# Which DMA engine a store leaves out: eleven dV by a table, and pairs of o in two or three parts

## The chip, the cores and the metric

The kernel runs on one core of one Trainium2 chip. The metric is the device time of one execution in microseconds (us); lower is better.

## The reference

The kernel computes attention and its gradients for 32 batches. Each batch has 32 query heads of 4 rows, so 128 rows of 128 elements, and 4 key/value heads of 2048 rows. All tensors are bf16.

```python
def _fwd_reference(q, k, v):            # q (32,32,4,128), k and v (32,4,2048,128)
    k = jnp.repeat(k, rep, axis=1)      # rep = 8 query heads for each key head
    v = jnp.repeat(v, rep, axis=1)
    scores = jnp.einsum("bhqd,bhkd->bhqk", q, k) * D ** -0.5
    p = _softmax(scores, axis=-1)
    return jnp.einsum("bhqk,bhkd->bhqd", p, v)

def reference(q, k, v, grad_out):
    out, vjp = jax.vjp(_fwd_reference, q, k, v)
    return (out, *vjp(grad_out))        # o, dQ, dK, dV
```

K and V are 2 MB each per batch, and so are dK and dV; q, grad_out, o and dQ are 32 KB each. The core reads 136 MB and writes 136 MB.

## The kernel before

One batch is one unit of work. Its 128 query rows lie on the 128 partitions, and K, V, dK and dV lie as 128 partitions of 4 heads by 16 rows by 128 elements: a partition holds 4 KB of each head, which is also contiguous in memory. A DMA of one of these tensors therefore moves rows of 4 KB, one for each partition and head.

The steps of a batch have short names. LK and LV load K and V, four DMAs of 512 KB each, issued by SyncE (lines 153 and 159). QDT, KT and VT turn q, K and V by TensorE's transpose through PSUM; VectorE copies them out (line 182). Sa and Sb compute the scores and their maxima, EXa and EXb the exponentials, NRM the sums, their reciprocals and two scaled operands, `dop` and `qp`, which GpSimd writes (line 230). ETa, ETb, dSTa and dSTb turn the exponentials and dS back. O computes the output and its inner product with grad_out, dPa and dPb compute dS. dV0 to dV7 and dK0 to dK7 (`outer`, lines 295 to 337) each compute an eighth of dV or dK into two PSUM banks, which ScalarE copies (line 310) into an output tile. dQ is the last step.

The order of all steps is written out by hand: HEAD for the first batches, STEADY for a loop body that works on a batch and its neighbours, TAIL for the end. Every engine executes its share in that order. K has three buffers, V two. dV and dK share four output tiles (`out_pool`, tag "outp"), so a tile is written again by the same tensor two batches later, after its store has landed.

Stores are issued by GpSimd through `store` (line 132), behind each other and between its other work; only after the last V load has been issued do they go to SyncE's queue. When the eighth dV or dK of a batch has been copied, its tile is stored at once (lines 326 to 337). Outputs o go out for two batches at a time, at each odd batch (lines 277 to 279). GpSimd also loads q and grad_out for four batches at a time (`GROUP`).

The stores of some batches are split by partitions ("rows" below). A store of 128 rows gives 8 rows to each of the 16 DMA engines. In the code's reckoning a store of fewer rows uses as many engines as the largest number up to 16 that divides its rows: 120 rows use 15 engines, 104 use 13, 88 use 11, 40 use 10, 24 use 12, 8 use 8. Those engines follow each other from a round-robin start, and the next such store starts where the last ended. Before the change dV of batch 0 is stored as 128 rows of two heads, then 88 and 40 rows of the other two, which puts the start at engine 5. At each fourth batch (3, 7, ... 27) dV is stored as 128 rows of one head, then 120 and 8 rows of the other three, and the pair of o before it (from batch 7 on) as 104 and 24 rows, so that the start is at 5 again. The 120 rows of these seven dV leave out engine 4.

Of the kernel before, what the change touches and what calls it, by code (L numbers as in the profile page):

```python
# [40 lines left out]
dV0@-1 dPa@-1 dV3@-1 dK4@-1 dQ@-2 dK3d@-1 dK2@-1 dK0d@-1 dK1@-1 dK5d@-1 dK7@-1 dK6@-1 dSTa@-1 dSTb@-1 dQ@-1  # L41
"""
TAIL_ITERATIONS = 3


class Banks:
# [31 lines left out]
def kernel(ctx: ExitStack, tc: tile.TileContext, q, k, v, grad_out, out_0, out_1, out_2, out_3):  # L78
# [3 lines left out]
    P = 128  # L82
# [38 lines left out]
    o_f = out_0.rearrange("b h s d -> b (h s) d")  # L121
# [3 lines left out]
    dk_v = out_2.rearrange("b h (p c) d -> b p h (c d)", c=C)  # L125
    dv_v = out_3.rearrange("b h (p c) d -> b p h (c d)", c=C)

    st = {}

    def store(**kw):  # L130

        (nc.sync if "v" in st.get(B - 1, {}) else nc.gpsimd).dma_start(**kw)  # L132
# [125 lines left out]
    def gathered(S, xt, kv):  # L258
        t = banks.take(1)
        ps = banks.ap(t)[:, 0, 0:D]  # L260
        for c in range(C):
            for h in range(NH):
                nc.tensor.matmul(  # L263
                    ps[G * h:G * h + G, :], lhsT=S[f"{xt}{c // 8}"][:, c % 8, G * h:G * h + G], rhs=S[kv][:, h, c, :],
                    start=(c == 0), stop=(c == C - 1), tile_position=(0, G * h),
                )
        return t, ps

    def O(b):
        S = st[b]  # L270
        t, ps = gathered(S, "et", "v")
        if b % 2 == 0:
            st["o"] = io_pool.tile([P, 2, D], BF16, name="o_sb")
        o_sb = st["o"][:, b % 2, :]
        nc.vector.tensor_scalar(out=o_sb, in0=ps, scalar1=S["rinv"][:], scalar2=None, op0=ALU.mult)
        banks.give(t)
        if b % 2:
            for r in (slice(0, 104), slice(104, P)) if b % 4 == 3 and b > 3 else (slice(0, P),):
                store(out=o_f[b - 1:b + 1, r].rearrange("w p d -> p w d"), in_=st["o"][r])
        junk = sm_pool.tile([P, D], BF16, name="junk")  # L280
        S["delta"] = sm_pool.tile([P, 1], FP32, name="delta")
        nc.vector.tensor_tensor_reduce(
            out=junk[:], in0=o_sb, in1=S["do"], scale=1.0, scalar=0.0,
            op0=ALU.mult, op1=ALU.add, accum_out=S["delta"][:],
        )
# [9 lines left out]
    def outer(S, x, y, dst, name, i, b, copy):  # L295

        if name not in S:
            S[name + "left"] = 8
            S[name] = out_pool.tile([P, NH, C, D], BF16, name=name, tag="outp")
        t = banks.take(2)  # L300
        ps = banks.ap(t).rearrange("p a (j c d) -> p a j c d", j=2, c=2)
        for c in range(2):
            u = P * ((2 * i + c) % 8)
            for a in range(2):
                r = slice(2 * G * a, 2 * G * a + 2 * G)
                nc.tensor.matmul(  # L306
                    ps[:, a, :, c, :], lhsT=S[f"{x}{i // 4}"][r, u:u + P], rhs=S[y][r, :, :],
                    start=True, stop=True, tile_position=(2 * G * a, 0),
                )
        copy(  # L310
            out=S[name][:, :, 2 * i:2 * i + 2, :].rearrange("p h c d -> p h (c d)"),
            in_=banks.ap(t).rearrange("p a (j w) -> p (a j) w", j=2),
        )
        banks.give(t)
        S[name + "left"] -= 1
        if b == B - 1:

            half = f"{name}half{i // 4}"
            S[half] = S.get(half, 4) - 1
            if S[half] == 0:  # L320
                c = slice(8 * (i // 4), 8 * (i // 4) + 8)
                store(
                    out=dst[b].rearrange("p h (c d) -> p h c d", d=D)[:, :, c, :].rearrange("p h c d -> p h (c d)"),
                    in_=S[name][:, :, c, :].rearrange("p h c d -> p h (c d)"),
                )
        elif S[name + "left"] == 0:
            o = S.pop(name)[:].rearrange("p h c d -> p h (c d)")
            parts = [(slice(0, P), slice(0, NH))]

            if name == "dv" and b == 0:
                parts = [(slice(0, P), slice(0, 2)), (slice(0, 88), slice(2, 4)), (slice(88, P), slice(2, 4))]
            elif name == "dv" and b % 4 == 3:
                parts = [(slice(0, P), slice(0, 1)), (slice(0, 120), slice(1, 4)), (slice(120, P), slice(1, 4))]
            for r, h in parts:
                store(out=dst[b][r, h, :], in_=o[r, h])

    def dV(b, i, copy=nc.scalar.copy):
        outer(st[b], "e", "dop", dv_v, "dv", i, b, copy)  # L340

    def dK(b, i, copy=nc.scalar.copy):
        outer(st[b], "ds", "qp", dk_v, "dk", i, b, copy)

    def dP(b, i):
# [6 lines left out]
        banks.give(t)  # L352

    table = {"LK": LK, "LV": LV, "QDT": QDT, "O": O, "dQ": dQ, "NRM": NRM}
    for i, c in enumerate("ab"):
        for n, f in (("S", S_), ("EX", EX), ("dP", dP), ("ET", ET), ("dST", dST)):
# [8 lines left out]
    for w in STEADY.split():  # L365
        ahead = 0
        for mark, n in (("+3", 3), ("+2", 2), ("+", 1), ("-2", -2), ("-", -1)):
            if w.endswith(mark):
                w, ahead = w[:-len(mark)], n
# [3 lines left out]
    with tc.manual_schedule():  # L373

        for w in HEAD.split():
            w, b = w.split("@")
            table[w](int(b))
        for it in range(HEAD_ITERATIONS, B - TAIL_ITERATIONS):
            for w, ahead in steady:
                if 0 <= it + ahead < B:  # L380
                    table[w](it + ahead)
        for w in TAIL.split():
            w, b = w.split("@")
# [31 lines left out]
```

## Time and profile before

| | |
|---|---|
| time of three runs, median (lowest to highest) | 685.96 us (685.48 to 688.05) |
| the profiled execution: its time | 682.75 us |
| its span from first to last instruction | 680.5 us |
| mean granted TensorE clock | 0.998 |
| TensorE matmul busy | 623.7 us, 92% of the span |
| VectorE, ScalarE, GpSimd busy | 594.5, 563.3, 259.6 us |
| moved by DMA | 274.45 MB, mean 403 GB/s |
| DMAs issued by SyncE, by GpSimd | 269, 140 |

The profile is one execution on the chip. The busy time of an engine is the sum of its instructions. The chain of waits is followed back from the last instruction: at each step to what released it, or to the instruction before it on the same engine. "DMA k_sb<-in_k_dram" in it is time in which the chain waits for a load of K. Queue q1 holds the DMAs issued by SyncE, q0 those issued by GpSimd, q8 and q14 fetch instructions. The DMA share is the mean busy share of the core's 16 DMA engines.

### The profile page before, as it was taken

The page shows a single profiled execution, that of the slowest core. Times are in us where ns is not written, and L with a number is a line of the kernel's source. Part 1 is how long each engine was busy: PE and PEld are TensorE (multiplying, and loading weights), DVE is VectorE, ACT ScalarE, POOL GpSimd, SP SyncE. Part 2 cuts the span into 40 slices and gives each one's busy share as a digit, 9 for nine tenths or more (in the row PEclk, how much of TensorE's full clock was granted, in tenths as well). Part 3 has the DMA queues.
Part 4 walks back from the last instruction along what each step waited for, and adds up shares of the span by engine and source line. Part 5 has one row for each costly group of instructions (what it writes and reads, how often), then busy time and mean ns, then how long its engine had stood idle before and what let it go on. Part 6 is the DMA issues. An engine that isn't in the chain of part 4 may idle for free.

```text
span 680.5 us, 27999 instructions
## 1 busy us (share of the span) xinstructions
PE 623.7 (92%) x12352; PEld 449.1 (66%) x12352; DVE 594.5 (87%) x1003; ACT 563.3 (83%) x666; POOL 259.6 (38%) x436
## 2 busy tenths in 40 slices
PE   5899999999999999988999999899999999899984
PEld 4577766667776667765667766577666677566652
DVE  4999999899899889889888889789898898898895
ACT  0599898898888888888988888888888888896885
POOL 1254243534424454432535324353244542344310
PEclk9999999999999999999999999999999999999999
DMA  8989999999999999999999999999999999999998
GB/s 326 406 293 400 416 417 411 416 413 416 416 414 417 412 417 415 416 416 415 416 416 414 416 414 417 414 411 416 414 417 398 409 414 416 415 401 406 370 368 317
DMA packets 76483, 274.45 MB, mean 403 GB/s; under 512 B 8579, under 2 KB 8651, under 8 KB 76361
## 3 DMA queue, kind: packets, MB, share of 16 engines
q1 hardware_dynamic: 42185, 145.11, 53.2%
q0 software_dynamic: 34176, 127.55, 46.6%
q8 instruction: 96, 1.57, 0.8%
q14 instruction: 26, 0.21, 0.1%
HBM read 136.31 MB, written 136.31 MB: 401 GB/s over the span
## 4 chain that ended last, share of the span: by engine, by line
PE 53%; DMA 36%; DVE 4%; ACT 3%; issue 2%; SPq 1%; POOL 0%; ACTq 0%; DVEq 0%; POOLq 0%
DMA k_sb<-in_k_dram 35%; PE banks L180 22%; PE banks L306 14%; PE banks L263 8%; PE banks L197 5%; PE banks L247 5%; ACT dv L310 2%; DVE kt L182 1%; DMA v_sb<-in_v_dram 1%; SPq L153 1%; DVE dk L310 1%; DVE m L210 1%; PE banks L170 1%; DVE ds L349 1%; DVE vt L182 0%
## 5 line engine op out<-in xcount | busy, mean ns | idle before, releaser
L310 ACT CAST dv<-banks 128x1024 bf16<-128x1024 f32 x254 | 244.4, 1025 | 47.7 <-PE banks L306 47.1
L310 ACT CAST dk<-banks 128x1024 bf16<-128x1024 f32 x251 | 246.0, 1022 | 29.9 <-PE banks L306 26.9
L182 DVE COPY kt<-banks 128x1024 bf16<-128x1024 bf16 x256 | 165.1, 680 | 9.9 <-PE banks L180 9.8
L182 DVE COPY vt<-banks 128x1024 bf16<-128x1024 bf16 x256 | 166.4, 680 | 2.6 <-PE banks L180 2.0
L180 PE MATMUL banks<-ident,k_sb 128*128 128x128 bf16 x2048 | 148.0, 221 | 18.5 <-DMA k_sb<-in_k_dram 13.3
L230 POOL TENSOR_SCALAR dop<-do_sb,rinv 32x128 bf16<-32x128 bf16 x124 | 74.2, 598 | 220.6 <-PE banks L306 125.2
L180 PE MATMUL banks<-ident,v_sb 128*128 128x128 bf16 x2048 | 143.5, 219 | 12.4 <-ACT dv L310 8.8
L180 PEld LDWEIGHTS <-k_sb 128*128 128x128 bf16 x2048 | 120.7, 99 | 48.4 <-issue 31.8
L180 PEld LDWEIGHTS <-v_sb 128*128 128x128 bf16 x2048 | 121.3, 98 | 28.2 <-issue 26.2
L306 PE MATMUL banks<-dop,e 64*128 64x256 bf16 x1024 | 97.6, 273 | 7.0 <-issue 4.3
L349 DVE SCALAR_TENSOR_TENSOR ds<-banks,delta,e 128x1024 bf16<-128x1024 f32 x64 | 82.0, 1283 | 17.1 <-PE banks L197 17.0
L306 PE MATMUL banks<-qp,ds 64*128 64x256 bf16 x1024 | 87.0, 272 | 2.6 <-DVE dk L310 1.1
L132 POOL DMA_DIRECT2D out_dram<-dv x46 | 32.5, 708 | 139.9 <-ACT dv L310 133.5
L230 POOL TENSOR_SCALAR qp<-q_sb,srinv 32x128 bf16<-32x128 bf16 x128 | 77.9, 609 | 10.7
L221 ACT ACTIVATE e<-banks,negb 128x1024 bf16<-128x1024 f32 x64 | 70.7, 1111 | 11.4 <-DVE negb L213 11.4
L210 DVE TENSOR_REDUCE m<-banks 128x1 f32<-128x1024 f32 x64 | 75.2, 1215 | 1.7 <-PE banks L197 1.5
L306 PEld LDWEIGHTS <-e 64*128 64x128 bf16 x1024 | 34.0, 94 | 52.9 <-issue 36.6
L249 DVE COPY et<-banks 128x1024 bf16<-128x1024 bf16 x64 | 41.4, 685 | 27.1 <-PE banks L247 27.0
L306 PEld LDWEIGHTS <-ds 64*128 64x128 bf16 x1024 | 40.8, 94 | 30.8 <-ACT dv L310 12.6
L249 DVE COPY dst<-banks 128x1024 bf16<-128x1024 bf16 x64 | 43.4, 679 | 0.0
L197 PE MATMUL banks<-vt,qdt 128*32 128x512 bf16 x512 | 41.3, 384 | 1.8 <-issue 1.6
L197 PE MATMUL banks<-kt,qdt 128*32 128x512 bf16 x512 | 39.6, 384 | 0.7 <-DVE vt L182 0.3
(40 smaller groups left out, 460.1 us busy)
## 6 DMA issues: line engine op xcount, KB each, us to landing
k_sb<-in_k_dram SPq DMA_DIRECT2D x128, 512.0 KB, 14.5
v_sb<-in_v_dram SPq DMA_DIRECT2D x128, 512.0 KB, 20.5
out_dram<-dk POOLq DMA_DIRECT2D x29, 2048.0 KB, 23.4
out_dram<-dv POOLq DMA_DIRECT2D x22, 2048.0 KB, 27.5
out_dram<-dv POOLq DMA_DIRECT2D x7, 1440.0 KB, 27.2
out_dram<-dk SPq DMA_DIRECT2D x2, 2048.0 KB, 10.3
out_dram<-dv POOLq DMA_DIRECT2D x7, 512.0 KB, 20.4
out_dram<-dv SPq DMA_DIRECT2D x1, 2048.0 KB, 12.0
```

The lines of the kernel that those rows point to most:

```text
L180: nc.tensor.transpose(out=ps[:, 4 * hh + j, :], in_=S[which][:, 2 * (i % 2) + hh, 4 * (i // 2) + j, :], identity=ident[:])
L182: nc.vector.tensor_copy(out=S[f"{which}t{i}"][:], in_=ps)
L197: nc.tensor.matmul(ps[G * h:G * h + G, a, :], lhsT=S["qdt"][:, col, G * h:G * h + G], rhs=xt[:, 4 * (h % 2):4 * (h % 2) + 4, :].rearrange( ...
L210: nc.vector.reduce_max(out=S["m"][:, i:i + 1], in_=S[f"s{i}"][1], axis=AX.X)
L221: nc.scalar.activation(out=S[f"e{i}"][:], in_=ps, func=ACT.Exp, bias=S["negb"][:], scale=scale, accum_out=S["l"][:, i:i + 1],)
L230: engine.tensor_scalar(out=t[r, h % 2, :], in0=src[r, :], scalar1=by[r, :], scalar2=None, op0=ALU.mult)
L247: nc.tensor.transpose(out=ps[:, u, :], in_=S[f"{src}{i}"][:, P * u:P * u + P], identity=ident[:])
L249: nc.vector.tensor_copy(out=S[f"{name}{i}"][:], in_=ps)
L263: nc.tensor.matmul(ps[G * h:G * h + G, :], lhsT=S[f"{xt}{c // 8}"][:, c % 8, G * h:G * h + G], rhs=S[kv][:, h, c, :], start=(c == 0), stop ...
L306: nc.tensor.matmul(ps[:, a, :, c, :], lhsT=S[f"{x}{i // 4}"][r, u:u + P], rhs=S[y][r, :, :], start=True, stop=True, tile_position=(2 * G * ...
L310: copy(out=S[name][:, :, 2 * i:2 * i + 2, :].rearrange("p h c d -> p h (c d)"), in_=banks.ap(t).rearrange("p a (j w) -> p (a j) w", j=2),)
L349: nc.vector.scalar_tensor_tensor(out=S[f"ds{i}"][:], in0=ps, scalar=S["delta"][:], in1=S[f"e{i}"][:], op0=ALU.subtract, op1=ALU.mult,)
```

## The change

A table names eleven batches, and for each the engine that the 120 rows of dV shall leave out and whether the 8 rows are stored ahead of the 120 or behind them. Seven of them are the batches split before, with engine 4; new are 9 and 17 (engine 6), 18 (engine 5) and 21 (engine 3). The split of dV of batch 0 is gone. The round-robin start is kept in `st["cursor"]`. At an odd batch of the table the pair of o is stored in two or three parts whose rows are chosen (`cut`) so that the start moves to where dV of that batch needs it; if it is there already, the pair is one store. With the 8 rows ahead, they start nine engines after the one to be left out, else one after it behind the 120. dV of batch 18 follows without a pair of o, with the start where batch 17 left it. At batch 31 the pair of o is one store instead of two. GpSimd issues 151 DMAs instead of 140.

```diff
+RELIEF = {3: (4, True), 7: (4, True), 9: (6, True), 11: (4, False), 15: (4, False), 17: (6, True), 18: (5, False), 19: (4, True), 21: (3, False), 23: (4, False), 27: (4, False)}
+def engines(rows):
+    return max(n for n in range(1, 17) if rows % n == 0)
+def cut(shift):
+    for a in range(8, 121):
+        for b in sorted({128 - a} | set(range(8, 121 - a)), reverse=True):
+            parts, at, load = [n for n in (a, b, 128 - a - b) if n], 0, [0] * 16
+            for n in parts:
+                for i in range(engines(n)):
+                    load[(at + i) % 16] += n // engines(n)
+                at += engines(n)
+            if at % 16 == shift and max(load) <= 12 and len(parts) == (2 if shift in (4, 5, 6, 7, 8, 9, 10, 13) else 3):
+                ends = [sum(parts[:i]) for i in range(len(parts) + 1)]
+                return list(zip(ends, ends[1:]))
+def begin(b):
+    engine, ahead = RELIEF[b]
+    return (engine + (9 if ahead else 1)) % 16
...
-    st = {}
+    st = {"cursor": 0}
...
         if b % 2:
-            for r in (slice(0, 104), slice(104, P)) if b % 4 == 3 and b > 3 else (slice(0, P),):
-                store(out=o_f[b - 1:b + 1, r].rearrange("w p d -> p w d"), in_=st["o"][r])
+            parts = [(0, P)]
+            if b in RELIEF:
+                if st["cursor"] != begin(b):
+                    parts = cut((begin(b) - st["cursor"]) % 16)
+                st["cursor"] = begin(b)
+            for r in parts:
+                store(out=o_f[b - 1:b + 1, slice(*r)].rearrange("w p d -> p w d"), in_=st["o"][slice(*r)])
...
             parts = [(slice(0, P), slice(0, NH))]
-            if name == "dv" and b == 0:
-                parts = [(slice(0, P), slice(0, 2)), (slice(0, 88), slice(2, 4)), (slice(88, P), slice(2, 4))]
-            elif name == "dv" and b % 4 == 3:
-                parts = [(slice(0, P), slice(0, 1)), (slice(0, 120), slice(1, 4)), (slice(120, P), slice(1, 4))]
+            if name == "dv" and b in RELIEF:
+                assert st["cursor"] == begin(b)
+                st["cursor"] = (begin(b) + 7) % 16
+                rows = [(slice(0, 120), slice(1, 4)), (slice(120, P), slice(1, 4))]
+                parts = [(slice(0, P), slice(0, 1))] + (rows[::-1] if RELIEF[b][1] else rows)
             for r, h in parts:
                 store(out=dst[b][r, h, :], in_=o[r, h])
```

## The prediction

> **What bounds the kernel now.** I read the load of the engines first, then the chain of waits, then the DMA queues, and last the single DMA packets. The windows (us busy, granted clock, DMA share, GB/s) show the two engines that matter:
>
> ```profile
> 60.00:250.00 190.00, 183.81 (x3731) 133.27 (x3729) 173.20 (x297) 169.34 (x201) 81.14 (x134) 1.00 1.03 415
> 260.00:600.00 340.00, 315.56 (x6372) 227.85 (x6372) 297.44 (x507) 289.61 (x344) 138.16 (x228) 1.00 1.03 414
> 600.00:650.00 50.00, 46.96 (x876) 30.44 (x861) 44.02 (x73) 41.83 (x51) 16.62 (x28) 1.00 0.98 390
> ```
>
> From 60 to 600 us all 16 DMA engines are busy all the time (the share is over 1 because the records of neighbouring packets overlap by 3 to 4 ns). TensorE is at 97% up to 250 us and 93% after. Which of the two ends last is in the chain of waits in order of time (start, us, what):
>
> ```profile
> 281.96 16.88 DMA k_sb<-in_k_dram
> ...
> 303.02 16.95 DMA k_sb<-in_k_dram
> ...
> 324.15 16.33 DMA k_sb<-in_k_dram
> ...
> 386.53 16.40 DMA k_sb<-in_k_dram
> ...
> 407.11 16.66 DMA k_sb<-in_k_dram
> ```
>
> Up to 260 us the chain has hardly a DMA in it, and a batch takes 19.6 to 20.3 us. From 260 us on each batch waits for its K, one batch per (407.11 - 281.96)/6 = 20.86 us. K stays the pace until the last V lands, at 648.4 us by the landing events; the 32 us behind that are compute and the last stores. So about (648 - 260)/20.86 = 18.6 batches are paced by the loads, and a load has landed only when the latest of 16 engines has done its rows. The queues in 260 to 600 us:
>
> ```profile
> q0 software_dynamic: 19013, 71.12, 51.8%
> q1 hardware_dynamic: 18856, 68.66, 49.8%
> q8 instruction: 50, 0.82, 0.9%
> ```
>
> Loads (q1, issued by SyncE) and stores (q0, issued by GpSimd) share the engines about half and half, and a third queue, instruction fetches, comes on top: 96 of 16 KB in the whole run.
>
> The packet records name no engine, but on one engine a packet starts 3 to 4 ns before the end recorded for the one before, so they can be strung together into 16 rows of packets. (A left-out engine is known by 24 packets of 4 B in place of rows: the numbers below are the table's.) 62 to 548 us gives:
>
> ```
> engine      fetches   stall in row packets   remark
> 4           0         25.6 us                left out in seven dV already
> 7 to 14     8-9 each  4.4 to 6.3 us          each fetch 0.95 us, then some 0.4 us of stall
> the others  0         2.4 to 5.9 us          5, 6 and 3 are among these
> ```
>
> Three facts follow. A 4 KB row takes 155.5 ns. The latest engines are 7 to 14: by 530 us they are 9 to 19 load packets behind the mean, and 4 swings by about 10 around it, forward after each dV that spares it. And from 260 us on 7 to 14 take one load packet, one store packet, one load packet with no exception in some 15,000 changes, a 4-byte completion write counting as a turn like a 4 KB row.
>
> The price of a batch on engine 7 follows. Loads: 8 DMAs of 8 rows and 1 completion are 72 turns, 64 x 155.5 + 8 x 6 ns = 10.00 us. Between them stand 72 store turns. From batch 11 to 28 its stores are 1307 turns of 188.0 us together (rows by 155.5 ns, small packets by their own), 143.8 ns a turn: 10.35 us. Fetches: 12 per engine over 32 batches by 1.35 us: 0.50 us. The sum, 20.85 us, is the measured pace.
>
> **The change, part by part.** *The seven dV that spare 4* stay at the same batches, so 4 keeps its relief of 21 rows (24 less 3) each; three (3, 7, 19) now send the 8 rows ahead, which moves 3 rows each from engines 4 to 11 to engines 13 to 4.
>
> *Four new ones* (9 and 17 spare 6, 18 spares 5, 21 spares 3) take work from engines that are not late. Directly they bring nothing, and they give 1 to 2 rows each to the others.
>
> *What they do to the turns* is the term I count. A split dV is 3 DMAs of 8+1, 24+1 and 3+1 turns, 38, where a whole one has 33; on engines outside the 8 rows the last 3 are of 4 B. From batch 11 to 28 there are 8 splits for 5, and two more parts of o (2 turns each): 3 x 5 + 4 = 19 turns more, 1326. The rows on the worst of 7 to 14 come to 188.5 us, so a store turn is 142.2 ns for 143.8. For 72 turns that is 10.24 us for 10.35, 20.74 for 20.85 us a batch: 0.115 x 18.6 = **2.1 us** off the loads' pace.
>
> By the Trainium skill ("DMA: Bandwidth & Descriptors", section "Queues, rings and completion order") an engine changes queue only after a whole packet, typically 9 to 17 descriptors. By that a small write would take no turn of its own and this term would be nothing. The trace here shows changes after single rows and single 4-byte writes, so I keep it.
>
> *The split of dV of batch 0 goes.* It gave engines 0 to 4 24 rows, 5 to 10 16, 11 to 15 8; now all have 16. Before 260 us the chain is TensorE's, so the rows moved there cost nothing; if that cover were gone, 8 rows are 1.2 us on engines 12 to 14, which stand 4 us better than 7 (141.8 against 143.7 ns a turn, 2088 turns), and 7 gains 1.0 us (143.5 to 142.3 ns, 792 turns). Both stay as bounds.
>
> *GpSimd's queue:* 151 DMAs for 140, at most two more issues by 0.71 to 0.75 us ahead of its next work, 1.5 us. Behind a dV store in its order stand the multiplies of NRM (dop, qp) and the stores of dQ and dK; dop waits for others anyway:
>
> ```profile
> POOL out_dram L132 <- ACT dv L310: 73.0, 16, 7.0
> POOL dop L230 <- PE banks L306: 65.8, 10, 7.3
> POOL dop L230 <- DVE rinv L238: 48.2, 7, 7.9
> ```
>
> That is 114 us in 17 waits, 6.7 us each, so 1.5 us is covered. Without cover it would be 1.5 us in each of the four new splits, 6 us at most.
>
> *SyncE's queue:* the last o is one store instead of two (an issue takes 0.39 us), beside compute: nothing, a gain of 0.4 us if it is not.
>
> Sum: 2.1 us off the profiled execution's 682.75 us (span 680.5 and 2.2 around it), 680.6 us. The median of the runs is 3.2 us above that execution; the same difference takes 685.96 to **683.9 us**. A measurement of this kernel (685.48 to 688.05 in three runs) can tell about 0.5%, 3.4 us, from no change, so I call this forecast "same".
>
> **Rivals.**
>
> *Same, by work alone.* If the loads only borrow the time from the stores and the stores then hold the pace, the rows of the latest engine decide: 28.7 rows above engine 15 on 7 and 8 before, 3.7 on 9 and 10 after. As the whole is fixed, the mean falls from 7.5 to -14.5 on the same scale: 21.2 above the mean becomes 18.2. Three rows by 155.5 ns are 0.5 us: 685.5 us. For it: dK's store lands only 0.5 to 4.4 us before its tile is written again (from batch 12 on, by landing events and first evictions). Against: no engine waits for a store's landing in this profile.
>
> *Slower: the stores become the longer queue.* Over batches 0 to 28 stores have 2099 turns, 72.4 a batch, just over the loads' 72; with the change 2119, 73.1. If out tiles are held up, the pace is 73.1 x (142.2 + 139) ns + 0.5 = 21.06 us, 0.21 us more than before, by 18.6 batches 3.9 us: 689.9 us. For it: a split dV lands 1 us later than its neighbours (29.3 to 30.2 against 28 to 28.5 us), and one dK has only 0.5 us to spare. Against: from batch 12 on these landings show no trend (dK 24.1 to 26.8), though 72.4 is already above 72. It decides once the landings have grown by some 2.5 us, the usual spare time of dK.
>
> *Faster.* The lead that engine 7 gains before 260 us reaches the end as well, and SyncE's 0.4 us too: 3.5 us, 682.4 us. For it: these engines never catch up once late. Against: until 260 us the loads end nothing, and 12 to 14 lose some of what 7 gains.
>
> *The split doesn't leave out what it says.* The cuts of o (98, 84, 65, 54 rows) move the round-robin start only if a DMA takes the largest number up to 16 that divides its rows. If one doesn't, every later dV spares a wrong engine and 4 stalls on: the five left from batch 11 on are 5 x 21 x 155.5 ns = 16 us on it, less about 6 us by which it is ahead of the latest: 696 us. Against: 104 and 24 rows show exactly 13 and 12 engines in this trace. The Trainium skill ("DMA: Bandwidth & Descriptors", section "Why a DMA increments its semaphore by 16 and not by 1") names an exception by which GpSimd's DMA may use all 16 with rows rounded up. The 4-byte packets of this trace do not show it for 120, 104, 88, 40, 24 or 8 rows.
>
> **How the numbers follow.** Turns as counted, 683.9: 0.42. Work alone, 685.5: 0.20. Faster, 682.4: 0.22. Stores' pace, 689.9: 0.12. Wrong engine, 696: 0.04. Faster by over 0.5% is the third case, 0.22; within, the first two, 0.62; slower, the last two, 0.16. The range takes in the first three with the runs' own spread of some 1.3 us either way, and reaches towards the stores' pace: 681.0 to 688.8 leaves out 0.04, most of 0.12 and the end of the third, under 0.2.
>
> **What would show it.** Right: the K pace in the chain between 280 and 600 us falls from 20.86 to about 20.75 us, the last V lands at about 646, dK's spare time shrinks but stays above zero, 24 packets of 4 B stand on engine 4 in the same seven batches, POOL issues 151 DMAs with its waits for ACT still there. The pace unchanged and landings later is work alone. ACT waiting for a DMA of dk or dv is the stores' pace. Engine 4 late by more than 19 load packets is the wrong engine. The forecast is wrong if the pace moves by over 0.2 us a batch either way.

## The result: 0.8% slower, and the profile after

| | before | after |
|---|---|---|
| seven runs each on one chip, median (lowest to highest) | 688.05 us (685.48 to 688.61) | 693.24 us (690.13 to 695.72) |
| profiled execution: time, span | 682.75, 680.5 us | 693.24, 691.4 us |
| mean granted TensorE clock | 0.998 | 0.987 |
| last V lands | 648.4 us | 651.3 us |

The ratio is 1.008, with an interval of 1.0053 to 1.0107. The forecast was 683.9 us, "same"; the result lies above its range, and 1.008 times the 685.96 us that the forecast started from, 691.4 us, does too. For every kernel below, the kernel before was measured beside it (medians of 685.32, 686.59 and 684.25 us in three groups), and its ratio is against that measurement. Ratios leave out slow executions, over 1.5% above the fastest of the same kernel, and medians don't.

**The load of the engines**, the same windows as before (us busy, granted clock, DMA share, GB/s):

```profile
60.00:250.00 190.00, 176.57 (x3535) 127.82 (x3522) 165.11 (x283) 161.30 (x192) 76.75 (x126) 0.98 1.02 411
260.00:600.00 340.00, 315.58 (x6229) 227.97 (x6227) 295.90 (x502) 288.11 (x340) 139.50 (x229) 0.99 1.02 406
```

From 60 to 250 us, where the prediction expected no change, TensorE has lost 7.2 us of its 183.8 us of work and its clock is under 1.

**The chain of waits** has changed its bound. The lines by engine, of before and then of after:

```profile
PE 53%; DMA 36%; DVE 4%; ACT 3%; issue 2%; SPq 1%; POOL 0%; ACTq 0%; DVEq 0%; POOLq 0%
```

```profile
PE 78%; issue 6%; DVE 5%; DMA 4%; ACT 3%; POOL 2%; SPq 0%; ACTq 0%; DVEq 0%; POOLq 0%
```

The K loads, which paced the chain before, are nearly gone from it; the last V lands only 2.9 us later, but the execution ends 10.5 us later. "Issue" went from 2% to 6%, and the chain of after in order of time (start, us, what) has its longest pieces here:

```profile
193.20 24.17 DMA out_dram<-dv
217.96 1.14 POOL out_dram L160 x2
219.11 8.47 issue
227.59 0.81 POOL out_dram L160
228.40 0.09 issue
228.49 0.60 POOL dop L258
...
386.82 1.14 POOL out_dram L160 x2
387.96 8.40 issue
...
528.61 3.30 issue
```

A store of dV, from its issue at 193.20 us to its landing, is followed by two stores issued on GpSimd, 8.5 us of waiting there, a third store and `dop`; at 387 us the two stores and the wait come again. These are the parts of dV of batches 9 and 17. (In the third piece, at 528.61 us, TensorE stands between two matmuls of one step and waits for nothing that the profile names. It goes on at 531.91 us, 1.5 us after a 16 KB instruction fetch has ended, so it was most likely waiting for its instructions.)

**The waits** name what is new (us in total, times, longest):

```profile
POOL out_dram L160 <- ACT dv L344: 137.4, 28, 9.3
...
POOL out_dram L160 <- DMA out_dram<-dk: 16.9, 2, 8.5
...
PE banks L340 <- POOL dop L258: 10.2, 6, 4.8
...
POOL out_dram L160 <- DMA out_dram<-dv: 6.2, 1, 6.2
PEld L208 <- DMA k_sb<-in_k_dram: 5.5, 4, 2.3
```

Before, no store on GpSimd waited for a DMA at all. Now three wait, 23.1 us, and TensorE waits 10.2 us for `dop`, where the list of before has:

```profile
PE banks L306 <- POOL dop L230: 1.3, 2, 1.1
```

**GpSimd's timeline** shows the place. Before, batch 9 (start, us, what; in brackets the idle time ahead and what ended it):

```profile
208.51 0.71 POOL L132 DMA_DIRECT2D out_dram<-o_sb  x1
...
213.91 0.75 POOL L132 DMA_DIRECT2D out_dram<-dv  x1 [3.17 <-ACT dv L310]
221.53 2.62 POOL L230 TENSOR_SCALAR dop<-do_sb,rinv 32x128 bf16<-32x128 bf16 x4 [6.87 <-PE banks L306]
```

After, the same batch:

```profile
208.32 1.87 POOL L160 DMA_DIRECT2D out_dram<-o_sb  x3
210.19 0.80 POOL L169 DMA_DIRECT2D q_sb<-in_q_dram  x1
210.98 0.77 POOL L169 DMA_DIRECT2D do_sb<-in_grad_out_dram  x1
217.96 1.14 POOL L160 DMA_DIRECT2D out_dram<-dv  x2 [6.21 <-DMA out_dram<-dv]
227.59 0.81 POOL L160 DMA_DIRECT2D out_dram<-dv  x1 [8.48 <-DMA out_dram<-dk]
228.49 2.63 POOL L258 TENSOR_SCALAR dop<-do_sb,rinv 32x128 bf16<-32x128 bf16 x4
```

The last part of dV waits until 227.59 us, and `dop`, which is written behind it, starts 7.0 us later than before. By the landing events dK of batch 8 landed 0.28 us ahead of that issue.

**Why a store waits for another store.** The DMAs of GpSimd's queue name eight completion semaphores, 111 to 118, strictly in turn; and over all profiles of this study, in 1,711 of GpSimd's DMAs, none was issued sooner than 0.28 us after the landing of the DMA eight earlier. So eight can be in flight, and the ninth waits. Before, the smallest distance was 2.34 us, so no issue was held up. In batch 9 of after the queue holds dV, dQ, dK of batch 8, three parts of o, q, grad_out, three parts of dV: the three parts face dV, dQ and dK of batch 8, and were issued 0.59, 0.74 and 0.28 us after these had landed. The trace's records of the instructions name the wait: the issue at 227.59 us waits for semaphore 111, that of dK of batch 8, and signals 111 itself; the issue at 217.96 us has an instruction just ahead of it that waits for its semaphore, 117, and batch 17 has the same. The wait is thus written into the program. The Trainium skill ("DMA: Bandwidth & Descriptors", section "Why a DMA increments its semaphore by 16 and not by 1") asks for one semaphore per slot in flight, since two DMAs that share one can't be told apart; with eight semaphores, a wait for the DMA eight earlier is what that asks for, and the trace agrees: no issue came sooner than 0.28 us behind that landing.

**Then the clock.** Windows of 6 us, of before and then of after:

```profile
224.00:230.00 6.00, 6.00 (x136) 3.56 (x134) 5.46 (x10) 5.23 (x6) 4.17 (x8) 1.00 1.02 404
230.00:236.00 6.00, 5.14 (x78) 3.26 (x75) 5.49 (x8) 5.10 (x6) 0.75 (x1) 1.00 1.03 418
```

```profile
224.00:230.00 6.00, 1.17 (x19) 1.00 (x17) 2.46 (x5) 0.64 (x1) 2.16 (x4) 0.95 1.03 408
230.00:236.00 6.00, 5.00 (x88) 2.48 (x87) 1.01 (x4) 2.94 (x3) 5.12 (x9) 0.50 1.01 399
```

TensorE stands for 4.83 and 1.00 us waiting for `dop`, and runs at half its clock: the clock records have 0.5 for 6.8 us here (from 229.44 us, just before the first of these waits ends), for 3.4 us behind the stop of batch 17 and for 3.4 us behind the wait at 528.61 us. The DMA share stays at 1.01 or more: the transfers don't stop, compute does.

How much later than before the store of dK of a batch is issued (us) shows that hardly any of it is given back:

| batch | before | after | later by |
|---|---|---|---|
| 8 | 207.8 | 207.6 | -0.2 |
| 9 | 227.9 | 234.9 | 7.0 |
| 10 | 248.0 | 256.4 | 8.4 |
| 12 | 288.4 | 297.8 | 9.3 |
| 16 | 371.8 | 379.3 | 7.5 |
| 17 | 393.3 | 403.7 | 10.4 |
| 19 | 434.2 | 446.2 | 12.0 |
| 23 | 518.5 | 528.6 | 10.1 |
| 24 | 539.2 | 552.7 | 13.5 |
| 27 | 601.7 | 613.1 | 11.4 |

Where it falls between the stops, it falls by about half a microsecond a batch (9.3 to 7.5 from 12 to 16, 12.0 to 10.1 from 19 to 23): TensorE, now the bound, is faster than the loads were, but at 91% busy hardly so. The 3.4 us that come at batch 24 follow the wait at 528.61 us; a like one (4.83 us at 110.68 us) stands in the profile of another kernel below, without the parts at 9 and 17, so it is not put down to the change. The profiled execution of before was also 2.7 us under the fastest of its runs here; the medians, 5.2 us apart, are the measure of the change.

### The profile page after: what moved, and what is told of

The parts are those of the page before. It is cut to its first block, busy times and chain, and to the rows that moved or that the text cites. A ratio compares the mean times of both kernels' runs of the same rounds, so it can differ in the third digit from the quotient of the medians.

```text
span 691.4 us, 28012 instructions
## 1 busy us (share of the span) xinstructions
PE 627.7 (91%) x12352; PEld 452.9 (66%) x12352; DVE 594.2 (86%) x1003; ACT 563.3 (81%) x666; POOL 266.7 (39%) x447
## 2 busy tenths in 40 slices
DMA packets 76794, 274.45 MB, mean 397 GB/s; under 512 B 8833, under 2 KB 8946, under 8 KB 76672
## 4 chain that ended last, share of the span: by engine, by line
PE 78%; issue 6%; DVE 5%; DMA 4%; ACT 3%; POOL 2%; SPq 0%; ACTq 0%; DVEq 0%; POOLq 0%
PE banks L208 31%; PE banks L340 20%; PE banks L291 9%; PE banks L225 9%; PE banks L275 7%; DMA out_dram<-dv 3%; ACT dv L344 2%; POOL dop L258 1%; DVE kt L210 1%; DVE m L238 1%; PE banks L198 1%; DMA k_sb<-in_k_dram 1%; DVE ds L381 1%; DVE dk L344 1%; DVE vt L210 1%
## 5 line engine op out<-in xcount | busy, mean ns | idle before, releaser
L208 PE MATMUL banks<-ident,k_sb 128*128 128x128 bf16 x2048 | 146.0, 221 | 16.0 <-issue 10.1
L340 PE MATMUL banks<-dop,e 64*128 64x256 bf16 x1024 | 99.1, 276 | 15.5 <-POOL dop L258 10.2
L160 POOL DMA_DIRECT2D out_dram<-dv x52 | 36.0, 696 | 164.9 <-ACT dv L344 137.4
L340 PE MATMUL banks<-qp,ds 64*128 64x256 bf16 x1024 | 88.5, 272 | 2.4 <-DVE dk L344 1.1
L340 PEld LDWEIGHTS <-ds 64*128 64x128 bf16 x1024 | 42.5, 94 | 30.0 <-ACT dv L344 12.6
```

The costliest lines, as they stand in the source:

```text
L208: nc.tensor.transpose(out=ps[:, 4 * hh + j, :], in_=S[which][:, 2 * (i % 2) + hh, 4 * (i // 2) + j, :], identity=ident[:])
L340: nc.tensor.matmul(ps[:, a, :, c, :], lhsT=S[f"{x}{i // 4}"][r, u:u + P], rhs=S[y][r, :, :], start=True, stop=True, tile_position=(2 * G * ...
```

## Experiments

The theory: eight DMAs can be in flight on GpSimd's queue; at batches 9 and 17 seven DMAs stand between dK of the batch before and the last part of dV, so that GpSimd stands until that dK has landed, `dop` is late, TensorE idles and then runs at half clock. Rivals: the parts cost by themselves (turns, issues, small packets); leaving out the wrong engines makes the loads late; the 8 rows ahead or the lost split of batch 0 cost; the stores become the longer queue. The first three were set against runs, the last against the trace of after; the engines 6, 5 and 3 were not tried one by one.

**Parts without any engine left out** (kernel before, only batches 9 and 17 changed; 96, 112 and 16 rows all use 16 engines):

```diff
-            for r in (slice(0, 104), slice(104, P)) if b % 4 == 3 and b > 3 else (slice(0, P),):
+            for r in (slice(0, 96), slice(96, 112), slice(112, P)) if b in (9, 17) else (slice(0, 104), slice(104, P)) if b % 4 == 3 and b > 3 else (slice(0, P),):
...
+            elif name == "dv" and b in (9, 17):
+                parts = [(slice(0, P), slice(0, 1)), (slice(0, 112), slice(1, 4)), (slice(112, P), slice(1, 4))]
```

> The kernel before, with dV and the pair of o of batches 9 and 17 stored in three parts each, as the change does, but in parts of 128, 112 and 16 rows (dV) and 96, 16 and 16 rows (o), so that all 16 DMA engines get the same rows and the round-robin start stays. Theory (completion lanes: a store of GpSimd waits until the store eight before it has landed, so the parts at 9 and 17 stop GpSimd ahead of NRM's multiplies, and TensorE runs dry): GpSimd waits for DMA out_dram in total 15 to 25 us at these two places as in the changed kernel, the granted clock falls below 0.99, and the time is 5 to 8 us above the kernel before. Rival (which engines are left out, and the turns, cost the time): no such waits and 688 us, within 1.5 us of the kernel before.

Measured: 690.13 us median, ratio 1.0069 (1.0037 to 1.0102), 4.8 us above the kernel before beside it, where 5 to 8 us were expected. The profiled execution took 700.41 us, so only its order of events is read:

```profile
222.09 1.26 POOL L132 DMA_DIRECT2D out_dram<-dv  x2 [3.83 <-DMA out_dram<-dv]
231.70 0.54 POOL L132 DMA_DIRECT2D out_dram<-dv  x1 [8.34 <-DVE vt L182]
232.32 2.63 POOL L230 TENSOR_SCALAR dop<-do_sb,rinv 32x128 bf16<-32x128 bf16 x4
```

TensorE waits for `dop` again:

```profile
PE banks L306 <- POOL dop L230: 7.0, 5, 3.0
```

The same picture: two parts, a long wait, the third part, `dop`. (The 8.34 us are put down to `vt`; the issue is 0.28 us behind the landing of dK of batch 8.) Leaving out other engines is not needed for the loss: it is there with none left out at 9 and 17.

**Half of it each.** If the parts cost by themselves, half of the parts costs half. If it is the place in the queue, three parts of o with a whole dV let dV face dV of the batch before, which lands 10 us sooner than dK; three parts of dV with a whole o let the last part face it. Both are the edit above with one of its two halves.

> The kernel before, with o of batches 9 and 17 in 96, 16 and 16 rows; dV stays one store. Half of the edit of the run with both in parts (ratio 1.0069). Lane theory (an issue of GpSimd waits for the landing of its DMA eight earlier): dV of 9 and 17 is then the eighth DMA behind dV of 8 and 16, so it is issued some 3 to 8 us later than before, but never faces dK of 8 or 16. One wait of GpSimd for a dV at each of the two places, none for a dK; TensorE waits for dop under 2 us in all; ratio 0.999 to 1.003. Rival (the parts themselves cost, each by its share): two of the four extra DMAs at each place, so half of the loss, 1.0035, and no such pattern of waits.

> The kernel before, with dV of batches 9 and 17 in 128 rows of one head, then 112 and 16 rows of three; o stays one store. Lane theory: only the last part of dV faces dV of 8 and 16, so one wait of GpSimd for a dV of 3 to 8 us at each of the two places, on the last part alone, none for a dK; TensorE waits for dop under 2 us in all; ratio 0.999 to 1.003. Rival (the parts themselves cost, each by its share): half of the loss of both, 1.0035.

Measured: o alone 685.43 us, ratio 1.0002 (0.9972 to 1.0032); dV alone 686.17 us, 1.0008 (0.998 to 1.0035). Neither alone is clear of no change, both together cost 0.7%. The times alone separate this from two equal halves only just: the intervals reach 1.0032 and 1.0035, and the medians lie 1.2 and 1.9 us above the 684.25 us beside them. The traces say more. GpSimd at batch 9, o alone and then dV alone:

```profile
218.46 0.76 POOL L132 DMA_DIRECT2D out_dram<-dv  x1 [6.95 <-DMA out_dram<-dv]
221.31 2.63 POOL L230 TENSOR_SCALAR dop<-do_sb,rinv 32x128 bf16<-32x128 bf16 x4 [2.09 <-PE banks L306]
```

```profile
215.28 1.27 POOL L132 DMA_DIRECT2D out_dram<-dv  x2 [3.16 <-ACT dv L310]
220.50 0.54 POOL L132 DMA_DIRECT2D out_dram<-dv  x1 [3.95 <-DMA out_dram<-dv]
223.91 2.62 POOL L230 TENSOR_SCALAR dop<-do_sb,rinv 32x128 bf16<-32x128 bf16 x4 [2.88 <-DVE rinv L238]
```

TensorE's wait for `dop`, o alone and then dV alone:

```profile
PE banks L306 <- POOL dop L230: 1.3, 2, 1.1
```

```profile
PE banks L306 <- POOL dop L230: 0.8, 1, 0.8
```

GpSimd waits for a DMA in both, for 6.95 and 3.95 us, on just the DMA that counting eight back names. But it is through 2 to 3 us before `dop`'s other inputs are there, and `dop` is not late: TensorE waits for it no longer than before. In the whole execution GpSimd waits 17.8 us for DMAs with o alone, not much under the 23.1 us of the kernel after. So the cost does not go by the length of the wait but by what is left of it when `dop` is due. One detail of the expectation failed: "none for a dK". The store of dK of batch 9, two places further back, faces dK of batch 8 (issued 0.57 us after its landing); it stands behind `dop`, and TensorE does not wait for it.

**The table without 9, 17 and 18** (the kernel after; 18 needs the start that 17 leaves):

```diff
-RELIEF = {3: (4, True), 7: (4, True), 9: (6, True), 11: (4, False), 15: (4, False), 17: (6, True), 18: (5, False), 19: (4, True), 21: (3, False), 23: (4, False), 27: (4, False)}
+RELIEF = {3: (4, True), 7: (4, True), 11: (4, False), 15: (4, False), 19: (4, True), 21: (3, False), 23: (4, False), 27: (4, False)}
```

> The kernel after with 9, 17 and 18 taken out of the table (18 needs the start that 17 leaves). Lane theory: no issue of GpSimd is within 0.9 us behind the landing of the DMA eight earlier, no wait of GpSimd for a DMA of out_dram over 2 us, granted clock never 0.5 between 100 and 600 us; the loss is gone, ratio 0.996 to 1.001. Rival (the entry of 21, or the 8 rows ahead at 3, 7 and 19, are part of it): 1.003 or more.

Measured: 684.74 us, ratio 0.9999 (0.9976 to 1.0021): the loss is gone. "No wait over 2 us" was wrong, and so was "no issue within 0.9 us" (there are seven):

```profile
POOL out_dram L160 <- DMA out_dram<-dv: 10.2, 2, 7.5
...
POOL out_dram L160 <- DMA out_dram<-dk: 3.1, 1, 3.1
...
PE banks L340 <- POOL dop L258: 3.0, 4, 1.1
```

At 11, 19 and 21 there are waits like those of the halves, and they are covered like those: TensorE waits for `dop` 1.1 us at most. One spell of half clock (6.8 us from 112.56 us) begins inside a wait of TensorE that the profile names no cause for (4.83 us at 110.68 us); no DMA of GpSimd is waited for there.

**The same table, the loads of q and grad_out one batch earlier.** All eleven entries stay, but the two loads no longer stand ahead of dV of 9 and 17: five DMAs between dK and the last part instead of seven. The same move in the kernel before is the control.

```diff
-        if b % W == W - 1 and b + 1 < B:
+        if b % W == W - 2 and b + 2 < B:
```

> The changed kernel with one step moved: GpSimd issues the loads of q and grad_out for the next four batches one batch earlier (in LK of batches 2, 6, 10 and so on), beside an even batch, which has no o and no split dV except 18. The table, all parts and all row shares stay. At batches 9 and 17 the store eight before the first part of dV is then an older, landed one; only the last part may still meet the store of dV of the batch before, for 2 to 3 us, which the 6.7 us that GpSimd waits ahead of dop cover. Theory (completion lanes): GpSimd's waits for out_dram fall from 23 us to under 4 us, the granted clock is back at 0.99 or more, and the time is at the kernel before or below, 682.5 to 686 us beside its 685.3. Rival (the table's choice of engines or the number of parts costs the time by itself): 690 us or more.

> The kernel before with the same move of the loads of q and grad_out alone. It is the control: if the move itself does nothing, 685.3 us within 1.5 us. If the move alone wins or loses time, what the changed kernel does with it has to be read against this run.

Measured: after with the move 687.46 us, ratio 1.0021 (1.0 to 1.0043); before with the move 684.79 us, 0.9973 (0.9952 to 0.9994). At batch 9 the last part of dV is now issued in time:

```profile
219.44 0.80 POOL L160 DMA_DIRECT2D out_dram<-dv  x1 [2.84 <-DMA out_dram<-dv]
223.07 2.63 POOL L258 TENSOR_SCALAR dop<-do_sb,rinv 32x128 bf16<-32x128 bf16 x4 [2.82 <-PE banks L340]
```

TensorE's wait for `dop` in the whole execution:

```profile
PE banks L340 <- POOL dop L258: 1.7, 2, 1.0
```

Three quarters of the loss against before are gone (1.008 to 1.0021), with every store of the table in place. Against its own control the table still costs 0.4% (687.46 by 684.79; the two intervals do not overlap). The expectation had it at the kernel before or below, and 1.0021 is a little above. Its chain has 7.15 us of "issue" at 381.85 us: at batch 17 the last part of dV still waits, now for dV of 16, and is issued 0.29 us after that landed. GpSimd's waits for DMAs are some 31 us in total, where the expectation had under 4 us. But TensorE waits only 1.7 us for `dop`, so what the remaining 0.4% consists of stays open.

**Fewer DMAs on GpSimd's queue.** dQ, q and grad_out of the kernel after go through SyncE:

```diff
-            GROUP(b // W + 1, nc.gpsimd)
+            GROUP(b // W + 1, nc.sync)
...
-        store(out=dq_f[b], in_=dq_sb[:])
+        nc.sync.dma_start(out=dq_f[b], in_=dq_sb[:])
```

> The changed kernel, with the stores of dQ and the loads of q and grad_out issued by SyncE instead of GpSimd, so that fewer of GpSimd's DMAs stand between a store and the one eight before it; the table and all parts stay. Theory (completion lanes): GpSimd no longer waits for out_dram, the granted clock is back at 0.998, and the time is at or below the kernel before, 684 to 688 us. Rival (the table itself costs the time): 692 to 694 us, like the changed kernel.

Measured: 705.68 us, ratio 1.028 (1.0235 to 1.0325). The waits did what the theory says (no issue of GpSimd is nearer than 11.6 us to the landing eight earlier), but the time says nothing on it, since the edit made a larger stop elsewhere:

```profile
SPq L327 <- ACT dq_sb L325: 295.5, 32, 15.7
```

SyncE's queue stands 295.5 us for dQ with the loads of K behind it, and packets under 512 B go from 8,833 to 19,841. The run decides nothing between theory and rival.

**The seven old entries alone, with the 8 rows ahead**, so without the split of batch 0, without parts in three, one form for all:

```diff
+RELIEF = {b: (4, True) for b in (3, 7, 11, 15, 19, 23, 27)}
```

> The changed kernel with a table of only the seven batches 3, 7, 11, 15, 19, 23 and 27, all leaving out engine 4 with the 8 rows ahead; batch 0 is not split. Each pair of o there has two parts, as before the change. Theory (completion lanes at 9 and 17): no waits of GpSimd for out_dram, 688 us within 1.5 us of the kernel before. Rival (the end of the split of batch 0, or the 8 rows ahead, cost the time): 691 to 694 us.

Measured: 683.5 us, ratio 0.9979 (0.9961 to 0.9997). The lost split and the 8 rows ahead together cost nothing; nothing waits for a DMA on GpSimd (smallest distance 2.74 us).

**No split at all** (kernel before, o and dV whole everywhere) prices what leaving out engine 4 is worth:

> The kernel before with no store split at all: 119 DMAs from GpSimd, every DMA engine gets the same rows. It prices what leaving out engine 4 is worth. If engine 4 is late by its stalls (25.6 us in 486 us, against 3.3 us won by each dV that spares it), the time rises by 6 to 12 us, to 694 to 700 us, with the chain waiting for K. If leaving it out is worth nothing, 688 us. The theory of the lanes says only that GpSimd does not wait for out_dram.

Measured: 698.64 us, ratio 1.0188 (1.0165 to 1.0212), 13.3 us over before, 1.9 us for each of the seven. The K loads are 49% of the chain, as against 35%. That engine 4's own stalls make the difference is argued from the 25.6 us of the prediction's table; no run left out another engine in its place.

**Another choice of rows**: the seven with engine 4, the loads earlier, and dV of 5, 9, 13 and 17 in two parts that spread the rows over several engines instead of leaving one out:

```diff
+RELIEF = {b: 4 for b in (3, 7, 11, 15, 19, 23, 27)} | {5: 88, 9: 40, 13: 63, 17: 88}
...
+                    parts = [(slice(0, RELIEF[b]), slice(0, NH)), (slice(RELIEF[b], P), slice(0, NH))]
```

> A version built on the lateness of the engines as the trace of before shows it: the loads of q and grad_out one batch earlier, the seven dV that leave out engine 4 with the 8 rows ahead, and four dV in two parts that start at engine 15: 88 and 40 rows (batches 5 and 17: 16 rows less each for engines 10 to 14), 40 and 88 (batch 9: 16 less for 4 to 8), 63 and 65 (batch 13: 12 less for 8 to 14); engines 15 and 0 to 3 get 16 rows more each time. No engine is left out for 6, 5 or 3. If the loads' pace is set by engines 7 to 14, the worst of them has some 35 rows less by 155.5 ns, 5 us: 679 to 682 us beside 685.3, and fewer waits for K in the chain. If only engine 4 matters and the fetches do not, it is no better than the seven alone, 683.5 us, or worse by the o in three parts.

Measured: 704.34 us, ratio 1.0246 (1.0198 to 1.0294), far above the 679 to 682 us of one theory and the 683.5 us of the other.

```profile
POOL out_dram L159 <- DMA out_dram<-dk: 34.1, 6, 7.4
POOL q_sb L168 <- DMA out_dram<-dk: 17.2, 5, 4.1
ACT dv L343 <- DMA out_dram<-dv: 16.9, 5, 6.0
ACT dk L343 <- DMA out_dram<-dk: 6.9, 6, 2.7
```

Here is the mark that the prediction named for the stores' pace, ScalarE waiting for a DMA of dV or dK, beside the waits of GpSimd. In the kernel after no copy of dV or dK waits so (ScalarE has one wait of 0.6 us for a DMA, at dQ), so the two mechanisms can be told apart in a profile. How the loss here divides between them was not taken apart.

**The two gains together**, the seven entries with the 8 rows ahead and the loads one batch earlier:

> The seven batches with engine 4 left out and the 8 rows ahead (ratio 0.998 alone), and the loads of q and grad_out for four batches issued one batch earlier (ratio 0.997 alone in the kernel before). If the two gains are of different kinds (rows on engines 7 to 11, and the order of GpSimd's queue) they add to 0.995, 682 us. If both are the same spare time in GpSimd's queue, 0.997 to 0.998. If the batch earlier brings the loads next to a dV in three parts, as in the table with nine more parts, a wait of GpSimd for a DMA appears and the ratio is 1.000 or more.

Measured: 683.97 us, ratio 0.9986 (0.9963 to 1.001). They do not show as a sum. Why is open: q and grad_out are issued within 0.3 to 1.0 us of a landing eight earlier in four of the groups, but so they are, in four groups, with the loads moved alone. The three versions (0.9973, 0.9979, 0.9986) can't be told from each other; the first two are faster than before by 0.2 to 0.3%, with intervals that end just under 1.

## Why the prediction was wrong, step by step

- **GpSimd's queue: the step that failed.** It priced an extra DMA at its issue, "two more issues by 0.71 to 0.75 us", and laid 1.5 us under the 6.7 us for which `dop` waits anyway. The issues were as long as that: the three parts of o took 1.87 us. The wait between them was missing: 6.21 and 8.48 us for landings eight places earlier. The cover was real, 6.87 us ahead of `dop` at batch 9 in the trace of before, and it did hide 6.95 and 3.95 us in the halves. The bound "6 us at most" came from issues alone and was no bound. The number could have been had from the profile of before: dK of batch 8 landed at 227.78 us; with 0.28 us and an issue of 0.81 us `dop` could not start before 228.9, 7.3 us behind its 221.53. It came 7.0 us late. For batch 17 the same working gives 396.1 against 386.32, 9.8 us. There the stop added only some 3 to 4.5 us (7.5 to 10.4 and 12.0 in the table): dK of 16 was issued 7.5 us later than before but landed at 396.1 us, 1.1 us later. The clue stood in the list of SyncE's own waits, which the prediction did not draw on:

```profile
SPq L159 <- DMA v_sb<-in_v_dram: 121.4, 74, 2.9
```

  A load of V on SyncE waits for an earlier load of V, 74 times. By its issues and landings that queue, too, has eight semaphores, and 86 of its 261 later DMAs are issued within 1 us of the landing eight earlier, none before it.

- **The bound, loads from 260 us on**: right for before. In after it no longer held, because compute fell behind the loads at batch 9. The mechanism was sought where the chain of before was, in the DMA engines, and the change struck TensorE in the part where the prediction said that the loads end nothing.

- **The turns, 2.1 us**: not refuted, not earned. With the loads moved, K lands every 20.81 us from batch 13 to 29 with the table and every 20.95 us without it (20.90 in before); the term was 0.115 us. The last V lands 1.3 us earlier. This is one profiled execution each, and that of the control was 4.4 us above its median, so it is no proof. And that kernel is still 0.4% slower than its control, so the loads' lead does not reach the end. The pace of after itself (21.09 us) says nothing on the term: the loads waited for compute.

- **The four new reliefs bring nothing directly**: no run shows a gain from them, and the table without three of them lies at 0.9999. **Batch 0 and the 8 rows ahead at nothing**: right in that they cost nothing; the run of the seven alone (0.9979) is even a little faster than before. The 3 rows for each split that were moved off engines 4 to 11 would fit that, but they were not separated from the rest.

- **The rivals.** The stores' pace had the right sign and 689.9 us, nearer than the forecast, by a mechanism that did not act, so that was luck: dK's spare time did not shrink to zero but grew, from 0.5 to 4.4 us to 8.5 to 14.1 us (from batch 12 on), because compute stood. Work alone and faster did not occur. The wrong engine did not occur: parts that leave out none show the same loss. What it would have cost was in the right region: no relief at all is 13.3 us, where five misplaced ones were put at 10. The case that came, a wait for a place in the queue, was not among them.

- **What would show it** had "151 DMAs with its waits for ACT still there". Both came true (137.4 us for ACT), and neither looked at the wait that mattered. The two signs that looked at the loads failed: the last V at 651.3 us for about 646, and K every 21.09 us for 20.75.

## What to carry to other kernels

Before a store is cut into parts, or a DMA is added to a queue, count how many DMAs stand between it and the one that has its semaphore, and compare that landing with the moment at which the next instruction behind it is due: the price begins with what is left over. Where a queue with long stores also feeds compute (here `dop` behind dV on GpSimd), small DMAs such as parts of o and loads of q use up places as large ones do, so move them away from the large stores. TensorE, 91% busy, gave a stop of 7 us back at about half a microsecond a batch; a stop that is small against the span can therefore still be in the end time.

## What the runs showed of the hardware

- **Eight DMAs in flight for each issuing queue** in these programs, by semaphores in turn, on GpSimd and on SyncE; the next one is issued 0.28 us or more (GpSimd) behind the landing of the eighth before it. On GpSimd the wait is an instruction's own wait for its semaphore, so it is a limit of these programs; how many DMAs the queue itself could hold is not shown.
- **Half clock after a stop.** With 4.83 and 1.00 us of idle TensorE came 6.8 us at 0.5, with 1.93 and 1.10 us (with little work between them) 3.4 us. The Trainium skill ("TensorE: Matmul & The Clock Gate", section "What's actually happening") has the clock halved after an idle window of about 3.4 us, windows running free: the records of 3,413 and 6,827 ns are one and two such windows, and the spells of the kernel after begin 50 and 89 windows behind its first. But a window need not be wholly idle here. In the profiles of this study, from 20 us on and up to the last 10 us, TensorE was busy for half or less (0.505 at most) of the 3.4 us ahead of each spell, and for more than half (0.508 or more) of the other windows at full clock, with one exception (0.44). This fits the single spells of 3.4 us that also stand in profiles without such a stop (two in that of the seven entries alone). Of the 6.8 us, 5.5 us held work, so some 2.7 us of it were lost, about half of the stop again.
- **Two edits that cost nothing alone can cost together.** The halves at 1.0002 and 1.0008 would make 1.001; both together are 1.0069, with an interval from 1.0037. The halves' own intervals reach 1.0032 and 1.0035, so it is TensorE's wait for `dop` (1.3 and 0.8 us, against 7.0) that tells them apart.
- **Stores that leave out engine 4 are worth 13.3 us** in this kernel: without them 1.0188, 1.9 us for each of the seven splits.
